# Four kinds of instruction get a larger margin in a list scheduler: squares of w2, splits of the signal, the gate's input, and the loads of the second feed-forward

## The chip, the cores and the metric

The kernel runs on one core of a Trainium2 chip. The metric is the device time of one launch in microseconds (us), the median of several runs. A core has five engines that each work through a queue of their own in the order in which the program was written: TensorE (PE, matrix products, with its weight loads shown apart as PEld), VectorE (DVE), ScalarE (ACT), GpSimd (POOL) and SyncE (SP). SP does no arithmetic here; it issues DMA transfers. POOL issues those transfers that add to what lies in DRAM. An instruction whose operand isn't there waits at the head of its queue, and everything behind it on that engine waits too.

## The reference

For x of shape 2048 x 1024 (sequence by features):

```
xn  = layernorm(x)
kv  = causal_conv4(k, shift_k) * v
y   = causal_conv2048(kv, ssm_k) + kv * ssm_D        # per feature, by FFT of length 4096
out = x + xn * y + silu(xn @ w1) @ w2                # w1: 1024 x 3584, w2: 3584 x 1024
```

All arrays are float32. The kernel computes its products with float16 pairs (a high and a low part), three matrix products for one.

## The kernel before, in words

**Two streams of work.** The feed-forward is nearly all of TensorE's work. Its first product (`steps`, lines 980 to 982) runs until 578 us, its second (`steps2`, lines 1123 to 1125) from 579.7 us to the end. For a large part of both a Strassen-Winograd scheme with seven products for eight is used (`units`, `units2`); between its products ScalarE and VectorE copy partial sums out of PSUM (`evacuate`, `evacuate2`), and TensorE can go on in a bank of PSUM only when the copy has been made. Beside it the long convolution runs in eight groups of 128 features: `gate` (short convolution and product with v), `signal_parts` (the signal is cut in four parts, each scaled and split into a float16 pair, and transposed by DMA), `stage1` (a first transform by matrix products, lines 1625 to 1627), `forward`, `product` and `inverse` (VectorE), `result_parts`, `stage1_inv` (lines 1813 to 1815) and `gated` (product with xn, then the output).

**The order is planned.** No engine's queue is written by hand. Some forty generators (`Stream`) offer operations (`Op`), each with an engine, an estimated duration and a margin. For the next operation of each stream the planner (`Order.prepare`, line 166) works out the time at which its operands are there by the plan's own estimates, and adds the margin:

```
s.at = max(t + op.margin, s.floor)      # line 176
t = max(self.free[s.head.eng], s.at)    # line 187
best = t - s.bias, t, s                 # line 189: the smallest t - bias is emitted next
```

So a margin removes and adds no instruction and no wait. It decides only how late in its engine's queue the operation is put: the planner takes it to be ready that much later, and other operations go in front. On the chip the operation starts when its engine comes to it and its semaphores allow it. The margins before the change are 0.15 us for an ACT instruction (`A`) and 0.3 us for a load (`L`).

**The four places that the change touches.**
- `square_w2` (line 1322): for each of 28 blocks of w2 (512 KB, loaded into one of two buffers, `wraw` and `w2n`) ScalarE squares the block and sums it up. A square frees its buffer for the next load. When all 28 are done, `norms_w2` (line 1327) derives the scale `tau`, and only then `load_w2` loads w2 again, to be split for the second product.
- `split` in `signal_parts` (line 1590): for seven of the eight groups, four parts each, ScalarE writes the high half into the tile `cm`, VectorE the low half, and SP issues two DMA transposes from `cm` into `sig`. There is one `cm`: a part's first instruction waits until the transposes of the part before have read it.
- `norm_rows` (line 1784): the gate's input, rows of x, is loaded into a tile of the ring `xg` (or into a free `ht`) by two transfers, and four ACT instructions of 128 x 128 subtract the mean. The next tile's loads are offered when these four have been emitted.
- `load_h` (line 1293): SP loads the activations of the first product, stored in DRAM, for the second: 160 tiles of `hs` and 56 of `hsf`, 256 KB each, into `wo`, twelve half tiles in turn. Each feeds twelve matmuls.

Of the kernel before, what the change touches and what calls it, by code (L numbers as in the profile page):

```python
# [15 lines left out]
AF = mybir.ActivationFunctionType  # L16
# [33 lines left out]
PRODUCTS = {"P1": ("A11", "B11"), "P7": ("S3", "T3"), "P6": ("S2", "T2"), "P2": ("A12", "B21"),  # L50
            "P5": ("S1", "T1"), "P3": ("S4", "B22"), "P4": ("A22", "T4")}
# [5 lines left out]
PLAIN = [j for j in range(NF) if j // 2 not in PAIRS]  # L57
# [62 lines left out]
class Order:  # L120
# [27 lines left out]
    def add(self, gen, bias, floor=0.0):  # L148
        s = Stream(gen, bias, floor)
        self.streams.append(s)  # L150
        self.advance(s)
# [151 lines left out]
def h3_ffn_kernel(ctx, tc, x, kp, vs, fs, shift, dskip, w1, w2, cfwd, cinv, out):  # L303
# [17 lines left out]
    def size(a):  # L321
        n = 1
        for s in a.shape[1:]:
            n *= s
        return n
# [4 lines left out]
    def A(f, o, ins, us=None, m=0.15):  # L330
        return Op("ACT", us or 1.02 * (0.16 + size(o) * 0.84e-3), 0.2, f, ins, [o], m)

    def T(f, o, ins, us, m=0.1):
        return Op("PE", us, 0.3, f, ins, [o], m)

    def L(o, i, m=0.3):
        n = size(o) * o.shape[0] * mybir.dt.size(o.dtype)
        return Op("SP", 0.4, 0.1, lambda: nc.sync.dma_start(o, i), [i], [o], m, n)

    def X(o, i, m=0.3, k=None):  # L340

        n = size(o) * o.shape[0] * mybir.dt.size(o.dtype)
        k = k or (1.2 if i.space == bass.MemoryType.DRAM else 3.0)
        return Op("SP", 0.65 + n / 240e3, 0.1, lambda: nc.sync.dma_start(o, i, transpose=True), [i], [o], m, k * n)
# [8 lines left out]
    def v_stt(o, a, s, b, op0, op1, **k):  # L353
        return V(lambda: nc.vector.scalar_tensor_tensor(o, a, s, b, op0=op0, op1=op1), o,  # L354
                 [a, b] + ([] if isinstance(s, float) else [s]), **k)

    def a_act(o, i, func, scale=1.0, bias=None, total=None):
        def f():
            kw = {} if bias is None else {"bias": bias}
            if total is not None:  # L360
                kw["accum_out"] = total
            nc.scalar.activation(o, i, func, scale=scale, **kw)  # L362
        ins = [i] + [s for s in (scale, bias) if s is not None and not isinstance(s, float)]
        p = A(f, o, ins)
        p.table = func if func in (AF.Silu, AF.Sqrt) else None
        p.busy += 0.07 * (len(ins) - 1) - 0.06 * (i.space == bass.MemoryType.PSUM)
        if total is not None:
            p.busy += 0.19
            p.writes.append(total)
        return p  # L370

    def split(hi, lo, src, scale, after=()):

        yield a_act(hi, src, AF.Copy, scale)
        yield v_stt(lo, src, scale, hi, MUL, SUB)
        for t in after:
            t.set()
# [3 lines left out]
    hsf = [{p[0]: dram.tile([4, P, NQ, 2, P], F16, name=f"hsf{p[0]}{b}") for p in PRODUCTS.values()} for b in range(2)]  # L381
    hs = [dram.tile([4, P, NF, 2, P], F16, name=f"hs{b}") for b in range(4)]
# [6 lines left out]
    mu = cst.tile([P, NT], F32, name="mu")  # L389
# [57 lines left out]
    def norm(ring, ss, ns, then, flags, margin=1.5):  # L447
# [27 lines left out]
        for t in flags[1]:  # L475
            t.set()


    def small(o, i, scale, ins=()):

        return Op("ACT", 0.2, 0.2, lambda: nc.scalar.activation(o, i, AF.Copy, scale=scale), [i, *ins], [o], 0.15)
# [110 lines left out]
    def turned(src, tok, name, i, bias):  # L592

        yield ft.ready
        pt, ptok = ft.tile([P, KH, P])

        def mm():
            for c in range(KH):
                nc.tensor.transpose(pt[:, c, :], src[:, c * P:(c + 1) * P], ident)
        yield T(mm, pt, [src], 0.44, m=0.3)  # L600
        flag["turned", name, i].set()
        if tok is not None:
            tok.set()
        o = factor(name)[:, i]
        after = (ptok, flag["x", 0, name]) + ((flag["rows", i],) if name in ("A11", "A12") else ())
        add(split(o[:, :, 0], o[:, :, 1], pt, XS, after), bias)
# [523 lines left out]
    def uses2():  # L1130

        yield 0, "P1"
        for u in range(len(tiles2)):
            for n in ("P7", "P6", "P2", "P5") if u + 1 < len(tiles2) else ("P6", "P7", "P5", "P2"):
                yield u, n
            if u + 1 < len(tiles2):
                yield u + 1, "P1"
            yield u, "P3"
            yield u, "P4"
# [153 lines left out]
    def load_h():  # L1293
        yield flag["factors"]
        for h in range(2):
            for c, t in [(c, t) for ts in TOGETHER[h] for c in range(NC) for t in ts]:
                yield wo.ready
                flag["h", h, t, c].what = o, _ = wo.tile([P, 4, 2, P], F16)
                yield L(o, hs[t // 4][t % 4][:, PLAIN[4 * c]:PLAIN[4 * c] + 4])
                flag["h", h, t, c].set()  # L1300
        for u, n in uses2():
            sp, q = tiles2[u]
            yield wo.ready
            flag["h2", u, n].what = o, _ = wo.tile([P, NQ, 2, P], F16)
            yield L(o, hsf[sp][PRODUCTS[n][0]][q])
            flag["h2", u, n].set()

    def squares_w2():
# [11 lines left out]
    flag["w2 squares"] = Token(2 * NP)  # L1320

    def square_w2(raw, tok, o):
        yield a_act(raw, raw, AF.Square, total=o)
        tok.set()
        flag["w2 squares"].set()

# [132 lines left out]
    def convolution(floor):  # L1459
# [3 lines left out]
        sp = ra.tile([P, 2, 8, 2, 2 * P], F32, name="spec")  # L1463
# [5 lines left out]
        acc = sig[:, 0]  # L1469
# [96 lines left out]
        def signal_parts():  # L1566

            for g in range(NG):
                yield flag["scales", g]
                kf, ktok = kfs[g]  # L1570
                sc, _ = scs[g]
                whole = [kparts[:, :, q].rearrange("p b t w -> p b (t w)") for q in range(2)]
                add(split(*whole, kf.rearrange("p b t w -> p b (t w)"), sc[:, 1:2], (ktok, flag["kparts", g])), CB)
                for t in TO:
                    there = acc16.rearrange("p b (i t) w -> p (b i) t w", i=2)[:, :, t]
                    two = [there[:, :, q * P:(q + 1) * P] for q in range(2)]
                    if g < BY_DMA:
                        yield py_r.ready
                        px, ptok = py_r.tile([P, 2, 2, P])

                        def mm():
                            for b in range(2):
                                for i in range(2):
                                    nc.tensor.transpose(px[:, b, i, :], acc[:, b, t + 4 * i, :], ident)
                        yield T(mm, px, [acc[:, :, t::4, :]], 0.44, m=2.0)
                        add(split(*two, px.rearrange("p b i w -> p (b i) w"), sc[:, 0:1], (ptok, flag["part", g, t])), CB)
                        continue
                    yield cm_r.ready
                    cm, ctok = cm_r.tile([P, 2, 2, 2, P], F16, 2)
                    yield from split(cm[:, 0], cm[:, 1], acc[:, :, t::4, :], sc[:, 0:1])  # L1590
                    flag["part", g, t].n = 2
                    for q, o in enumerate(two):
                        yield X(o, cm[:, q].rearrange("p b i w -> p (b i w)"))
                        ctok.set()
                        flag["part", g, t].set()
# [188 lines left out]
        def norm_rows():  # L1784

            for g in range(NG):
                for t in TO:
                    r = more["xg"]
                    yield lambda: r.ready() or flag["quads", 1]() and hts.ready()
                    xgs[g, t] = xg, _ = (r if r.ready() else hts).tile([P, 2, 2, P], uses=2)  # L1790
                    for b in range(2):
                        yield L(xg[:, b], x4[b][:, :, t, g * P:(g + 1) * P])
                    for b in range(2):
                        for i in range(2):
                            n = b * T2 + 4 * i + t
                            yield a_act(xg[:, b, i], xg[:, b, i], AF.Identity, -1.0, mu[:, n:n + 1])
                    flag["xg", g, t].set()

        def stage1_inv():
# [48 lines left out]
        for gen, bias in ((loads(), 0.05), (load_v(), 0.04), (gate(), 0.04), (signal_parts(), CB), (stage1(), 0.02),  # L1848
                          (transforms(), 0.02), (squares_w2(), 0.0), (rest(floor), 0.0)):
            add(gen, bias, floor)  # L1850
# [65 lines left out]
    add(feed_forward(), 0.0)  # L1916
    add(load_x(), 0.06)
    add(load_h(), 0.05)
    add(room(), 0.05)
    add(change(), 0.1)  # L1920
# [43 lines left out]
```

## Time and profile before

| | us |
|---|---|
| time, median of 3 runs (lowest, highest) | 1244.58 (1244.14, 1245.72) |
| the profiled execution's own time | 1244.12 |
| its span | 1242.0 |
| PE busy in the span | 1227.1 (99%) |
| DVE busy | 1107.2 (89%) |
| ACT busy | 775.7 (62%) |

The profile is that of one execution. The span goes from the first instruction to the last; 2.1 us of the execution's time lie around it. The granted clock of TensorE was full, 0.999 in the mean. A row of the timeline reads: start, duration, engine, line, operation, what it writes and reads, shapes; in brackets how long the engine had stood idle before it, and who ended that. A row of the waits reads: who waited for whom, then microseconds in total, how many times, and the longest. Most lines of ACT and DVE are those of a helper (362 for ACT, 354 and 351 for DVE, 338 for loads), so the names of the tiles tell the instructions apart.

### The profile page before, as it was taken

The page shows a single profiled execution, that of the slowest core. Times are in us where ns is not written, and L with a number is a line of the kernel's source. Part 1 is how long each engine was busy: PE and PEld are TensorE (multiplying, and loading weights), DVE is VectorE, ACT ScalarE, POOL GpSimd, SP SyncE. Part 2 cuts the span into 40 slices and gives each one's busy share as a digit, 9 for nine tenths or more (in the row PEclk, how much of TensorE's full clock was granted, in tenths as well). Part 3 has the DMA queues.
Part 4 walks back from the last instruction along what each step waited for, and adds up shares of the span by engine and source line. Part 5 has one row for each costly group of instructions (what it writes and reads, how often), then busy time and mean ns, then how long its engine had stood idle before and what let it go on. Part 6 is the DMA issues. An engine that isn't in the chain of part 4 may idle for free.

```text
span 1242.0 us, 16865 instructions
## 1 busy us (share of the span) xinstructions
PE 1227.1 (99%) x6044; PEld 596.2 (48%) x6044; DVE 1107.2 (89%) x1248; ACT 775.7 (62%) x1357; POOL 83.3 (7%) x93
## 2 busy tenths in 40 slices
PE   9999999999999999999999999999999999999998
PEld 8544444444444544445444544544444454444454
DVE  7999996996999779998899799899989979997981
ACT  7868997886688897559752732753363374554351
POOL 0000000000000000000000000001030130123123
PEclk9999999999999999999999999999999999999999
DMA  9598989899799899879986558489576784888776
GB/s 369 127 315 265 322 301 325 262 258 217 233 346 291 241 309 295 244 205 315 297 269 153 155 186 171 122 293 278 125 168 169 178 170 141 180 150 133 164 142 97
DMA packets 277700, 278.77 MB, mean 224 GB/s; under 512 B 85616, under 2 KB 204656, under 8 KB 276336
## 3 DMA queue, kind: packets, MB, share of 16 engines
q1 hardware_dynamic: 261888, 261.17, 70.2%
q0 software_dynamic: 15728, 16.52, 10.3%
q8 instruction: 47, 0.77, 0.3%
q14 instruction: 37, 0.30, 0.1%
HBM read 171.46 MB, written 88.34 MB: 209 GB/s over the span
## 4 chain that ended last, share of the span: by engine, by line
PE 70%; DVE 19%; DMA 4%; issue 3%; ACT 2%; SPq 0%; DVEq 0%; ACTq 0%
PE ff L980 10%; PE ff L981 10%; PE ff L982 10%; PE ff L1123 10%; PE ff L1124 10%; PE ff L1125 10%; DVE spec L351 7%; DVE tmp L351 2%; DVE wo L354 2%; DVE sig L354 1%; PE ps L1625 1%; PE ps L1627 1%; PE ps L1626 1%; DMA wraw<-in_w 1%; DVE x L354 1%
## 5 line engine op out<-in xcount | busy, mean ns | idle before, releaser
L1123 PE MATMUL ff<-x,wo 128*128 128x512 f16 x868 | 328.1, 378 | 2.0 <-ACT hf L362 0.9
L1125 PE MATMUL ff<-x,wo 128*128 128x512 f16 x868 | 328.1, 378 | 0.0
L1124 PE MATMUL ff<-x,wo 128*128 128x512 f16 x868 | 328.1, 378 | 0.0
L980 PE MATMUL ff<-x,wo 128*128 128x512 f16 (+1 forms) x808 | 302.8, 375 | 3.3 <-ACT hf L362 3.3
L982 PE MATMUL ff<-x,wo 128*128 128x512 f16 (+1 forms) x808 | 302.8, 375 | 0.0
L981 PE MATMUL ff<-x,wo 128*128 128x512 f16 (+1 forms) x808 | 302.8, 375 | 0.0
L351 DVE TENSOR_TENSOR spec<-spec 128x1024 f32<-128x1024 f32 (+2 forms) x232 | 259.3, 1146 | 2.0
L1125 PEld LDWEIGHTS <-wo 128*128 128x128 f16 x868 | 84.9, 98 | 101.6
L1124 PEld LDWEIGHTS <-wo 128*128 128x128 f16 x868 | 84.9, 98 | 101.3 <-issue 3.3
L1123 PEld LDWEIGHTS <-wo 128*128 128x128 f16 x868 | 85.8, 99 | 98.6
L982 PEld LDWEIGHTS <-wo 128*128 128x128 f16 x808 | 79.0, 98 | 92.4 <-DVE wo L354 0.5
L981 PEld LDWEIGHTS <-wo 128*128 128x128 f16 x808 | 79.0, 98 | 92.0 <-issue 3.9
L980 PEld LDWEIGHTS <-wo 128*128 128x128 f16 x808 | 80.5, 100 | 88.1
L351 DVE TENSOR_TENSOR tmp<-spec 128x2048 f32<-128x2048 f32 (+1 forms) x48 | 92.5, 1934 | 1.0
L354 DVE SCALAR_TENSOR_TENSOR ht<-hf,wsc,ht 128x1024 f16<-128x1024 f32 (+1 forms) x56 | 67.2, 1203 | 19.6 <-ACT ht L362 19.6
L362 ACT ACTIVATE spec<-spec 128x1024 bf16<-128x1024 f32 x32 | 33.7, 1053 | 59.6 <-DVE spec L351 59.5
L354 DVE SCALAR_TENSOR_TENSOR wo<-raw,wsc,wo 128x1024 f16<-128x1024 f32 (+1 forms) x56 | 63.9, 1147 | 4.4 <-ACT wo L362 4.0
L362 ACT ACTIVATE wo<-raw,wsc 128x1024 f16<-128x1024 f32 (+1 forms) x56 | 57.7, 1033 | 11.7 <-DVE raw L351 8.8
L354 DVE SCALAR_TENSOR_TENSOR sig<-kin,taps,sig 128x1024 f32<-128x1024 f32 x48 | 61.5, 1281 | 2.5 <-ACT sig L362 2.4
L348 POOL DMA_DIRECT2D out<-hf x44 | 39.3, 906 | 342.7 <-ACT hf L362 280.4
L351 DVE TENSOR_TENSOR spec<-tmp 128x512 f32<-128x512 f32 (+1 forms) x80 | 61.3, 794 | 1.1
L362 ACT ACTIVATE ht<-hf,wsc 128x1024 f16<-128x1024 f32 (+1 forms) x56 | 60.6, 1084 | 2.2 <-DVE hf L351 1.0
(191 smaller groups left out, 1695.3 us busy)
## 6 DMA issues: line engine op xcount, KB each, us to landing
wo<-hs SPq DMA_DIRECT2D x160, 256.0 KB, 3.6
hs<-ht SPq DMA_DIRECT2D x80, 256.0 KB, 4.7
raw<-in_w SPq DMA_DIRECT2D x28, 512.0 KB, 5.9
wraw<-in_w SPq DMA_DIRECT2D x24, 512.0 KB, 5.6
w2n<-in_w SPq DMA_DIRECT2D x24, 512.0 KB, 6.2
ws_T<-wo SPq DMA_DIRECT2D x22, 512.0 KB, 5.8
kin<-in_kp SPq DMA_DIRECT2D x16, 704.0 KB, 6.0
wo<-ws_T SPq DMA_DIRECT2D x22, 512.0 KB, 4.7
```

The source lines that it names most:

```text
L348: return Op("POOL", 1.1, 3.0, lambda: nc.gpsimd.dma_start(o, i, accum_op=ADD), [i], [o], m, 2.3 * n)
L351: return V(lambda: nc.vector.tensor_tensor(o, a, b, op=op), o, [a, b], **k)
L354: return V(lambda: nc.vector.scalar_tensor_tensor(o, a, s, b, op0=op0, op1=op1), o, [a, b] + ([] if isinstance(s, float) else [s]), **k)
L362: nc.scalar.activation(o, i, func, scale=scale, **kw)
L980: nc.tensor.matmul(o, w[:, 0, k], xf[:, :, k, 0], start=first and k == 0, stop=False, **kw)
L981: nc.tensor.matmul(o, w[:, 0, k], xf[:, :, k, 1], start=False, stop=False, **kw)
L982: nc.tensor.matmul(o, w[:, 1, k], xf[:, :, k, 0], start=False, stop=last and k == KH - 1, **kw)
L1123: nc.tensor.matmul(po, hx[:, n, 0, :], wc[:, n, 0, :], start=first and n == 0, stop=False, **kw)
L1124: nc.tensor.matmul(po, hx[:, n, 0, :], wc[:, n, 1, :], start=False, stop=False, **kw)
L1125: nc.tensor.matmul(po, hx[:, n, 1, :], wc[:, n, 0, :], start=False, stop=last and n == 3, **kw)
L1625: nc.tensor.matmul(o, cf[:, 0], h, start=i == 0, stop=False, **kw)
L1626: nc.tensor.matmul(o, cf[:, 0], l, start=False, stop=False, **kw)
```

## The change

Two things are added: a helper that raises an operation's margin, and an argument of `split` for it. Four kinds of operation get more margin: the squares of w2 4 us more, the high halves of `cm` 3 us more, the mean's subtraction in `norm_rows` 4 us more, and the loads of `load_h` 3.0 us in place of 0.3. The other uses of `split` keep their margin (`wait=0.0`).

```
-    def split(hi, lo, src, scale, after=()):
-        yield a_act(hi, src, AF.Copy, scale)
+    def split(hi, lo, src, scale, after=(), wait=0.0):
+        yield later(a_act(hi, src, AF.Copy, scale), wait)
...
+    def later(op, us):
+        op.margin += us
+        return op
...
     def load_h():
-                yield L(o, hs[t // 4][t % 4][:, PLAIN[4 * c]:PLAIN[4 * c] + 4])
+                yield L(o, hs[t // 4][t % 4][:, PLAIN[4 * c]:PLAIN[4 * c] + 4], 3.0)
...
-            yield L(o, hsf[sp][PRODUCTS[n][0]][q])
+            yield L(o, hsf[sp][PRODUCTS[n][0]][q], 3.0)
...
     def square_w2(raw, tok, o):
-        yield a_act(raw, raw, AF.Square, total=o)
+        yield later(a_act(raw, raw, AF.Square, total=o), 4)
...
     def signal_parts():
-                    yield from split(cm[:, 0], cm[:, 1], acc[:, :, t::4, :], sc[:, 0:1])
+                    yield from split(cm[:, 0], cm[:, 1], acc[:, :, t::4, :], sc[:, 0:1], wait=3)
...
         def norm_rows():
-                            yield a_act(xg[:, b, i], xg[:, b, i], AF.Identity, -1.0, mu[:, n:n + 1])
+                            yield later(a_act(xg[:, b, i], xg[:, b, i], AF.Identity, -1.0, mu[:, n:n + 1]), 4)
```

## The prediction

> **What bounds the kernel now.** I read the page's busy times first, then TensorE's waits.
>
> ```profile
> span 1242.0 us, 16865 instructions
> PE 1227.1 (99%) x6044; PEld 596.2 (48%) x6044; DVE 1107.2 (89%) x1248; ACT 775.7 (62%) x1357; POOL 83.3 (7%) x93
> ```
>
> ```profile
> PE ff L980 <- ACT hf L362: 3.3, 2, 2.3
> PE ft L599 <- DVE x L354: 1.9, 3, 1.2
> PE py L1814 <- DVE zl L354: 1.7, 3, 1.1
> PE ft L1891 <- DVE one L408: 1.2, 1, 1.2
> PE ff L1123 <- ACT hf L362: 0.9, 2, 0.5
> PE ft L599 <- DVE xt L580: 0.8, 1, 0.8
> PE ff L1123 <- DVE hf L354: 0.6, 1, 0.6
> PE ff L1123 <- ACT ff L362: 0.4, 1, 0.4
> PE py L1584 <- DVE sig L354: 0.4, 1, 0.4
> ```
>
> TensorE is busy for 1227.1 of 1242.0 us, and these nine rows are all its waits: 11.2 us. Nothing in the change shortens a matmul, so the time can fall only by what is in this list. The third thing to see is what the list lacks: TensorE never waits for a DMA. It waits for ACT and DVE, so a late transfer reaches it only through them. The rows of lines 599, 1891 and 1584 (4.3 us) belong to the start, ahead of any moved instruction. What the change can reach is 3.3 + 1.7 + 0.9 + 0.6 + 0.4 = 6.9 us.
>
> A wait counts for a little more than its row. Matmuls overlap, and the next rows, TensorE's timeline at its worst stop and at two others, show by how much.
>
> ```profile
> 337.86 0.38 PE L981 MATMUL ff<-x,wo 128*128 128x512 f16 x1
> 338.07 0.38 PE L982 MATMUL ff<-x,wo 128*128 128x512 f16 x1
> 340.74 0.38 PE L980 MATMUL ff<-x,wo 128*128 128x512 f16 x1 [2.28 <-ACT hf L362]
> ...
> 354.86 0.38 PE L980 MATMUL ff<-x,wo 128*128 128x512 f16 x1 [1.02 <-ACT hf L362]
> ...
> 1074.54 0.38 PE L1123 MATMUL ff<-x,wo 128*128 128x512 f16 x1 [0.41 <-ACT ff L362]
> ```
>
> Matmuls of 512 columns start 0.21 us apart (337.86, 338.07) though each is shown for 0.38. Without a stop the one at 340.74 would have come at 338.28; it lost 2.46, the idle 2.28 plus 0.17. I add 0.17 to every stop.
>
> **What ACT was doing then.** ACT's waits for transfers, and its timeline around the three stops:
>
> ```profile
> ACT cm L362 <- DMA sig<-cm: 24.7, 11, 5.9
> ACT ht L362 <- DMA ht<-in_x: 15.8, 6, 5.6
> ACT xg L362 <- DMA xg<-in_x: 12.6, 4, 6.2
> ACT wraw L362 <- DMA wraw<-in_w: 8.3, 5, 5.7
> ```
>
> ```profile
> 337.41 1.06 ACT L362 ACTIVATE wraw<-wraw 128x1024 f32<-128x1024 f32 x1 [5.74 <-DMA wraw<-in_w]
> 338.47 0.58 ACT L362 ACTIVATE ff<-ff 128x512 f32<-128x512 f32 x1
> ...
> 353.18 1.06 ACT L362 ACTIVATE wraw<-wraw 128x1024 f32<-128x1024 f32 x1 [0.61 <-DMA wraw<-in_w]
> ...
> 354.24 0.58 ACT L362 ACTIVATE hf<-ff 128x512 f32<-128x512 f32 x1
> ...
> 1067.60 0.72 ACT L362 ACTIVATE cm<-sig,csc 128x512 f16<-128x512 f32 x1 [1.96 <-DMA sig<-cm]
> ...
> 1073.92 0.57 ACT L362 ACTIVATE ff<-ff 128x512 f32<-128x512 f32 x1
> ```
>
> The first four rows are 61.4 us of ACT standing still for exactly the transfers that the change's ACT instructions read. Most of it costs nothing: ACT is 62% busy. Three of these waits had a copy out of PSUM behind them on which TensorE depended. At 331.7 ACT begins to wait 5.74 us for w2 to be squared, and behind that square (1.06 us, its sum besides) stands the copy of 338.47 (`ff<-ff`). At 353.18 the third square, after 0.61 of waiting, stands in front of the copy of 354.24. At 1067.60 ACT loses 1.96 us at `cm`, then works without a break to the copy of 1073.92; TensorE's stop there is shorter than that wait.
>
> **The change, part by part.** No instruction is added, removed or resized; busy times stay. What moves is 28 squares with their 28 sums, 128 subtractions on `xg` or `ht` (8 groups, 4 tiles, 4 each), 28 high halves of `cm`, and 216 loads on SP. With these go, later in the plan, what hangs on them: 28 low halves on DVE and 56 transposes on SP behind `cm`, the 28 loads of w2 (each needs the buffer that a square frees), and the 64 half loads of x. POOL's transfers are not moved by it; they are behind the convolution's last step, and I come to that under the rivals.
>
> *Squares and subtractions, at 331 to 355 us.* The squares go 4 us back; the copies of 338.47 and 354.24 pass them. Both stops fall away: (2.28 + 0.17) + (1.02 + 0.17) = 3.64 us.
>
> *`cm`, 3 us back.* The wait of 1.96 is passed by the copies behind it: 0.41 + 0.17 = 0.58 us. The other `cm`, `xg` and `ht` waits have no TensorE stop behind them: gain 0.
>
> *Loads of h, 2.7 us back.* No gain on TensorE, since it waits for no DMA. On SP they stop blocking others:
>
> ```profile
> SPq L338 <- PE ff L1125: 251.7, 140, 8.7
> ```
>
> ```profile
> wo<-hs SPq DMA_DIRECT2D x160, 256.0 KB, 3.6
> ```
>
> SP stands 140 times, 251.7 us in all, until a matmul frees a tile; transposes and other loads behind can now pass. That may shorten the waits above, which are already at zero in the sum: gain 0, and not a loss either. The cost side: twelve half tiles, each feeding twelve matmuls of 0.21 us, are a round of 31 us. Less 3.6 us to land, less the longest SP wait of 8.7, at least 18 us are left between landing and use. 2.7 us of them cost nothing.
>
> [...]
>
> *What covers the delays of the others.* These rows are the last square, tau, the first split of w2 that needs tau; the fourth `cm` of the tightest group, and the transform that reads it; the last subtraction of the first group and the product that uses it:
>
> ```profile
> 480.72 1.06 ACT L362 ACTIVATE w2n<-w2n 128x1024 f32<-128x1024 f32 x1 [0.29 <-DMA w2n<-in_w]
> ...
> 488.03 0.18 DVE L1343 TENSOR_SCALAR tau<-tau 128x14 f32<-128x14 f32 x1
> ...
> 553.94 1.15 ACT L362 ACTIVATE x<-wraw,tau 128x1024 f16<-128x1024 f32 x1 [0.84 <-PE ff L982]
> ...
> 979.02 0.71 ACT L362 ACTIVATE cm<-sig,csc 128x512 f16<-128x512 f32 x1
> ...
> 1005.19 0.38 PE L1625 MATMUL ff<-sig,cfw 128*128 128x512 f16 x1
> ...
> 384.18 0.97 ACT L362 ACTIVATE xg<-xg,mu 128x128 f32<-128x128 f32 x3
> ...
> 434.57 0.69 DVE L351 TENSOR_TENSOR xg<-py,xg 128x512 f32<-128x512 f32 x1
> ```
>
> ```profile
> DMA to landing us min/median/max: 2.4/3.6/8.9
> ```
>
> The squares run from 337 to 482 us through two buffers, 14 rounds. If each round grows by the whole 3.85 us, tau comes 54 us later, at 542. It is not used before 553.94, where ACT waited for TensorE and not for w2; with 6 us for loading, 60 of those 66 us are free. Cost 0, but not by much. `cm`: the four parts of a group are one chain, so the fourth comes up to 12 us later. In the tightest group 26.2 us lie between it and its matmul; less 2.7 for the two halves and the second transpose's issue, less 8.9 for the slowest landing (the row above is that of the transposes from `cm`), 14.6 are left. Cost 0. `xg`: four tiles in a chain, up to 16 us; 50 are there.
>
> **The sum.** 3.64 + 0.58 = 4.2 us less for the profiled execution: 1244.12 - 4.2 = 1239.9. The median of the runs lies 0.46 above that execution, so 1240.4. What is late next are stops that hang on VectorE's turn from one group to the next (the 1.7 us on `zl`) and the two of 0.9; I leave them as they are. Without any of the 6.9 us, with 0.17 for each of nine stops, 8.4 us would go; less the one of 0.6 + 0.17, which is the tail between the last two products and stays, 7.6: 1237.0, the low end. Upward, every queue after 331 us is dealt anew. A stop like the largest (2.45) that appears elsewhere costs its length; the sum's own range is one either way that stays faster, 1237.0 to 1242.0.
>
> **The rivals.**
>
> *Given back.* The new order puts other ACT or DVE work in front of PSUM copies; stops of the size of these return. For it: five of the nine stops have nothing to do with transfers and sit where the groups turn. Against: between 355 and 1060 us there are, with ACT waiting in nearly every window, only the `zl` stops. A move of 2 to 4 us given back is 1242.1 to 1247.0, no change that can be told: about 0.2%, 2.5 us, is what a measurement of this kernel can tell from none.
> [...]
>
> *The change doesn't do what it says.* If in the plan nothing else was ready, the moved instructions keep their places: 1244.6. Against it, at 338.47 a ready copy did stand behind.
>
> *Tau comes too late (slower).* If the rounds of squares grow not by 3.85 but by over 4.3 us (say because w2's loads fall behind loads of factors in SP's queue), tau passes 548 us, and the splits of w2, which feed the second product from 579.7 on, start late. TensorE takes the first block 25.7 us after that split (579.7 in the row below); loading and splitting a block fills some 12 of these (6 to land, four instructions of about 1.2), so 14 us more are hidden, and it decides from a round 5.3 us longer; at 5.8 it costs 14 x 0.5 = 7 us less the 4.2 gained: 1247.4.
>
> ```profile
> L1123 PE MATMUL ff<-x,wo x868: 269/379/380, 579.7 to 1237.9; 128*128 128x512 f16 x172, 128*128 128x256 f16 x2
> ```
>
> *The convolution ends late (slower).* The rows of its last output and of the last unit's copy:
>
> ```profile
> 1214.23 1.72 POOL L348 DMA_DIRECT2D out<-ht  x1
> ```
>
> ```profile
> 1224.72 0.69 ACT L362 ACTIVATE hf<-ff,invc 128x512 f32<-128x512 f32 x1 [4.49 <-PE ff L1125]
> ```
>
> The last unit loads back what the convolution added (flag `conv out`) right behind that copy. If the four `cm` of a group come over 14.6 us later, VectorE loses the rest in each group, and from 10.5 us in total TensorE's last products wait, us for us. Three us in six groups would be 18 - 10.5 - 4.2 = 3.3 us slower: 1247.9. Against: 12 is the plan's whole shift, and the waits of 24.7 us at `cm` are part of it already.
>
> *A load of h comes late.* It needs 16 us more than planned; a stop of that kind, once, is 1244 to 1256. Nothing in TensorE's list points to it.
>
> **How the numbers follow.** The sum 0.58; given back 0.17 and no effect 0.03; tau 0.09; convolution 0.08; new stops beyond what is gained, or a load of h, 0.05. So faster 0.58, same 0.20, slower 0.22. The range 1237.0 to 1248.0 takes in the sum, the middle and the nearer half of the slower cases.
>
> **What will show it.** Up to 331 us the two timelines should be the same. Right: no TensorE stop at 331 to 360, ACT waits for `wraw`, `xg`, `ht` and `cm` well under 61 us, ff L980 <- ACT near 0, tau between 490 and 545, the last output by POOL near 1214. Wrong: a DMA among TensorE's releasers, tau after 560, or new stops on `hf`, `ff` or `zl` that add up to over 4 us.

## The result, and the profile after

The changed kernel takes 1239.51 us (median of 6 runs, 1238.87 to 1242.08), the kernel before 1244.53 (6 runs): a ratio of 0.9959, with a 95% interval of 0.9943 to 0.9975. The forecast was 1240.4. The profiled execution of the changed kernel took 1241.13 us, 1.6 above the median, with a span of 1239.1; so the two profiles, 1242.0 and 1239.1, show only 2.9 of the 5 us.

The same views of the changed kernel. Its lines stand 3 to 5 lower in the file: 980 is 985, 1123 is 1128, 1814 is 1819. First the page, then TensorE's waits:

```profile
span 1239.1 us, 16865 instructions
PE 1226.6 (99%) x6044; PEld 595.9 (48%) x6044; DVE 1107.3 (89%) x1248; ACT 775.6 (63%) x1357; POOL 83.3 (7%) x93
```

```profile
PE py L1819 <- DVE zl L354: 1.8, 1, 1.8
PE ft L604 <- DVE x L354: 1.5, 2, 1.2
PE ft L604 <- DVE xt L585: 1.2, 1, 1.2
PE ft L1896 <- DVE one L408: 1.2, 1, 1.2
PE ff L985 <- ACT hf L362: 0.7, 1, 0.7
PE ff L1128 <- DVE hf L354: 0.6, 1, 0.6
PE py L1589 <- DVE sig L354: 0.4, 1, 0.4
PE ff L1128 <- ACT hf L362: 0.3, 1, 0.3
PE ff L985 <- DVE hf L351: 0.2, 1, 0.2
```

Every engine is busy for as long as before, to within 0.5 us. What shrank is the list: the rows of the start are still 4.3 us, the tail's is still 0.6, and of the 6.3 us between them 3.0 are left. The largest row of before, 3.3 on a copy by ACT at the first product, is 0.7.

Where that row came from, ACT's timeline again:

```profile
333.40 0.58 ACT L362 ACTIVATE ff<-ff 128x512 f32<-128x512 f32 x1 [0.71 <-PE ff L987]
335.93 0.69 ACT L362 ACTIVATE hf<-ff,wsc 128x512 f32<-128x512 f32 x1 [1.95 <-PE ff L987]
...
338.48 1.06 ACT L362 ACTIVATE wraw<-wraw 128x1024 f32<-128x1024 f32 x1 [0.68 <-DMA wraw<-in_w]
...
346.29 0.58 ACT L362 ACTIVATE hf<-ff 128x512 f32<-128x512 f32 x1
```

```profile
346.92 0.38 PE L985 MATMUL ff<-x,wo 128*128 128x512 f16 x1 [0.67 <-ACT hf L362]
```

The copy whose end ended the stop of before, from the timeline of that kernel:

```profile
340.02 0.67 ACT L362 ACTIVATE hf<-ff,wsc 128x512 f32<-128x512 f32 x1
```

The copy `ff<-ff`, which stood behind the first square at 338.47, now runs at 333.40, as soon as TensorE has made its input; the square comes after it and waits 0.68 us in place of 5.74. The next copy, `hf<-ff`, stood behind the first two squares at 340.02 and now runs at 335.93. The stop of 2.28 us is gone. A shorter one is new: a copy at 346.29 stands behind two instructions of the convolution.

Part of the gain is given back at one place. TensorE's and VectorE's timelines at the turn to the third group, first both of the changed kernel, then both of the kernel before:

```profile
684.25 0.27 PE L1818 MATMUL py<-zh,civ 128*128 128x256 f16 x1
686.33 0.27 PE L1819 MATMUL py<-zl,civ 128*128 128x256 f16 x1 [1.80 <-DVE zl L354]
```

```profile
684.99 2.48 DVE L354 SCALAR_TENSOR_TENSOR zl<-spec,csc,zh 128x1024 f16<-128x1024 f32 x2
```

```profile
687.10 0.27 PE L1813 MATMUL py<-zh,civ 128*128 128x256 f16 x1
687.67 0.27 PE L1814 MATMUL py<-zl,civ 128*128 128x256 f16 x1 [0.29 <-DVE zl L354]
```

```profile
686.33 2.48 DVE L354 SCALAR_TENSOR_TENSOR zl<-spec,csc,zh 128x1024 f16<-128x1024 f32 x2
```

TensorE comes to this place 2.85 us earlier than before (684.25 against 687.10), VectorE only 1.34 (684.99 against 686.33). So TensorE stands there for 1.80 us where it had stood for 0.29. VectorE is busy for 89% of the span, and at the groups' turns it is the engine that TensorE waits for (`zl`: 1.7 us in three stops before, 1.8 in one now).

### The profile page after: what moved, and what is told of

It is laid out like the page before. It is cut to its first block, busy times and chain, and to the rows that moved or that the text cites. A ratio compares the mean times of both kernels' runs of the same rounds, so it can differ in the third digit from the quotient of the medians.

```text
span 1239.1 us, 16865 instructions
## 1 busy us (share of the span) xinstructions
PE 1226.6 (99%) x6044; PEld 595.9 (48%) x6044; DVE 1107.3 (89%) x1248; ACT 775.6 (63%) x1357; POOL 83.3 (7%) x93
## 4 chain that ended last, share of the span: by engine, by line
PE 67%; DVE 21%; DMA 5%; issue 4%; ACT 2%; SPq 1%; DVEq 0%; ACTq 0%
PE ff L1128 11%; PE ff L1130 11%; PE ff L1129 11%; PE ff L985 8%; PE ff L986 8%; PE ff L987 8%; DVE spec L351 6%; DVE ht L354 2%; DVE tmp L351 2%; DVE x L354 2%; DVE sig L354 2%; DVE wo L354 2%; PE ps L1631 1%; PE ps L1630 1%; PE ps L1632 1%
```

## The experiments

Three theories. Theory 1 is the prediction's: what counts is a copy out of PSUM that stood behind an ACT instruction waiting for a transfer, so the squares carry the gain and the rest gives next to nothing. Theory 2: the loads of h, put later, unblock SP's queue and so bring all transfers earlier. Theory 3: any new order gains or loses a few us by chance.

The runs in one table. The third column is ACT's waits in the profile for the four kinds of transfer that the change concerns (`cm`, `xg`, `ht`, and the squares' `wraw` and `w2n`), the last what TensorE stood idle between 300 and 1226 us, summed over the rows of its waits. The first two rows are from the measurement above. The others were measured on three chips, each against the kernel before on the same chip, where that takes 1243.0 to 1243.1 us.

| what moves | ratio (interval) | ACT's waits, us | TensorE idle, us |
|---|---|---|---|
| nothing (before) | 1 | 61.7 | 6.3 |
| all four parts | 0.9959 (0.9943 to 0.9975) | 16.9 | 3.0 |
| all four parts, again | 0.9963 (0.995 to 0.9977) | 20.6 | 1.8 |
| squares by 4 | 0.9966 (0.9954 to 0.9978) | 53.7 | 2.2 |
| first four squares by 4 | 0.9981 (0.9969 to 0.9993) | 56.1 | 3.0 |
| squares by 2 | 1.0004 (0.9991 to 1.0016) | 52.8 | 5.9 |
| squares and subtractions by 4 | 0.9956 (0.9942 to 0.997) | 24.6 | 0.4 |
| subtractions by 4 | 0.9998 (0.9988 to 1.0009) | 35.7 | 5.6 |
| `cm` by 3 | 1.0004 (0.9995 to 1.0014) | 43.8 | 5.3 |
| loads of h by 2.7 | 1.0018 (1.001 to 1.0027) | 64.6 | 7.5 |
| loads of h by 5.7 | 0.9997 (0.9988 to 1.0007) | 66.3 | 4.8 |
| all but the squares | 1.0018 (1.0008 to 1.0028) | 18.7 | 6.0 |
| squares by 10 | 1.0299 (1.0284 to 1.0315) | 67.0 | 38.6 |
| squares by 4, `cm` by 9 | 1.0072 (1.0058 to 1.0085) | 41.7 | 2.2 (a stop of 10.1 comes after 1226) |

**Each part alone.** Four kernels, in each of which one of the four margins is that of the changed kernel and the others are those of before:

```
 sq_only:  later(a_act(raw, raw, AF.Square, total=o), 4)                           # the rest 0, 0, 0.3
 xg_only:  later(a_act(xg[:, b, i], ..., AF.Identity, -1.0, mu[:, n:n + 1]), 4)
 cm_only:  split(cm[:, 0], cm[:, 1], ..., sc[:, 0:1], wait=3)
 h_only:   L(o, hs[...], 3.0) and L(o, hsf[...], 3.0)
```

> Only the squares of w2 keep their 4 us; the other three have the margins of before. Theory 1 (the gain is the copies out of PSUM that stood behind a square): both stops of 331 to 355 us go, 3.6 us less than before, about 1240.9; ACT's wait for wraw falls from 8.3 to under 2 us. Theory 2 (the gain is SP's queue, unblocked by the later loads of h): about 1244.5. Theory 3 (any new order gains or loses a few us by chance): anything within 4 us of before, and the four single parts don't add up to the 5.0 us of all.

> Only the subtractions on xg and ht keep their 4 us. Theory 1: no TensorE stop stood behind one of them, so within 1 us of before, 1243.5 to 1245.5, though ACT's waits for xg and ht fall from 28.4 us to a few. Theory 2: no change. Theory 3: up to 4 us either way.

> Only the high halves of cm keep their 3 us. Theory 1: one stop of 0.58 us goes, about 1244.0. Theory 2: no change, 1244.5. Theory 3: up to 4 us either way.

> Only the loads of h keep their margin of 3.0 us. Theory 1: 0, about 1244.5; SP's wait for PE at line 338 falls well under 251.7 us. Theory 2: most of the 5.0 us gained, about 1240, by shorter ACT waits for transfers. Theory 3: up to 4 us either way.

The squares alone give 0.34%, 4.2 us, all of the change's gain within the intervals. TensorE's waits after 300 us in that kernel, the tail left out, have no row at the first product:

```profile
PE py L1819 <- DVE zl L354: 0.7, 1, 0.7
PE ps L1630 <- ACT tmp L362: 0.6, 1, 0.6
PE ff L1128 <- ACT hf L362: 0.4, 1, 0.4
PE ps L1630 <- DVE tmp L351: 0.3, 1, 0.3
PE ff L1128 <- DVE hf L354: 0.2, 1, 0.2
```

Subtractions and `cm` alone make no difference, though ACT's waits fall from 61.7 to 35.7 and 43.8 us. The loads of h alone cost 0.18%, 2.2 us. TensorE's three largest waits in that kernel:

```profile
PE ff L985 <- ACT hf L362: 3.1, 2, 2.6
PE py L1819 <- DVE zl L354: 1.9, 1, 1.9
PE py L497 <- ACT spec L362: 1.6, 1, 1.6
```

The first row is the old stops, the other two are new or larger. The timelines of ACT, VectorE and TensorE at the third, all of the kernel with the loads of h alone:

```profile
882.14 0.72 ACT L362 ACTIVATE cm<-sig,csc 128x512 f16<-128x512 f32 x1 [3.90 <-DMA sig<-cm]
883.33 1.06 ACT L362 ACTIVATE spec<-spec 128x1024 bf16<-128x1024 f32 x1 [0.47 <-DVE spec L351]
```

```profile
882.00 1.29 DVE L351 TENSOR_TENSOR spec<-tmp 128x512 f32<-128x512 f32 x2
```

```profile
884.53 0.39 PE L497 MATMUL py<-css,one 128*128 128x4 f32 x2 [1.56 <-ACT spec L362]
```

A small matmul of the convolution needs ACT's sum of squares of the product (`spec`), and the whole of the second product stood behind this matmul in TensorE's queue. In ACT's queue the sum stands behind a `cm` that waited 3.90 us, but that isn't what held it: after the `cm` ACT stood idle for 0.47 us more, until VectorE had made `spec` at 883.29. VectorE has no row in this kernel's list of waits between 870 and 900 us. So this stop is not of the kind that the change takes away; TensorE came ahead of VectorE, as at `zl`.

Theory 2 falls: SP's wait at line 338 for a matmul of the second product fell from 251.7 to 191.1 us, and nothing was gained. Theory 3 is not out: the single ratios add up to -0.14%, the four together give -0.41 and -0.37. With the intervals of the four parts that sum is uncertain by some 0.2% either way, so the difference lies at the edge of the noise.

**All but the squares, and the loads of h by more.**

```
 no_sq:  cm 3, subtractions 4, loads of h 3.0, squares 0
 h_6:    only the loads of h, 6.0 in place of 3.0
```

> The changed kernel with the squares back at their old margin; cm, xg and h keep theirs. If the squares carry the gain (they gave 3.7 us alone): both or most of the 3.6 us of stops at 331 to 355 us return and the time is that of before within 1.5 us. If the other three carry something together that none shows alone (the four single ratios add up to -0.14%, all four together to -0.41%): 2 to 4 us faster than before. By the h part's own theory (loads of h later make ACT wait longer for the transposes from cm, 37.5 us against 24.7, unless cm moves too) the ACT wait for cm is under 20 us here.

> Only the loads of h move, by 5.7 us in place of 2.7 (2.7 alone: 2.3 us slower than before). If the loss comes with the delay (ACT's wait for cm, or a late load): larger, 3 to 6 us slower. If it was the chance of one order: anything between 2 us faster and 3 slower, and not larger with the margin. SP's wait for PE at line 338 falls below 191 us.

Without the squares nothing is gained; 0.18%, 2.2 us, is lost, somewhat more than the 1.5 us that I had allowed, though ACT's waits are at 18.7 us, among the lowest of all. TensorE's list doesn't show where (6.0 us against 6.3); the profiled execution, 1243.53 us, was one of the shortest of this kernel, 1.7 below its median. So the three parts don't carry the gain in company either, and the sum of ACT's waits says nothing about the time: 53.7 us of them are left in the kernel with the squares alone, which is as fast as the whole change. With the loads of h moved by twice as much the loss of 0.18% isn't there. So it doesn't come with the delay, nor with ACT's wait for `cm`, which is 37.8 us here and was 37.5 in the kernel that lost. That it was the chance of one order is what is left, and isn't shown. SP's wait fell further, to 149.1 us, and again nothing was gained.

**Two smaller doses of the squares.**

```
 sq_first:  later(..., 4) for the first four squares, 0 for the other 24
 sq_2:      later(..., 2) for all 28
```

> Only the first four of the 28 squares move, by 4 us; all else has the margins of before. Theory 1 (the gain is the two stops at 338 and 353 us, behind the first and third square): the whole gain of the squares, 3.6 us, and tau within 10 us of 488, not 527. If the gain is spread over the squares, or comes from the later loads of w2 that a later square brings: under half of it, 1.8 us.

> All 28 squares move by 2 us in place of 4. The first copy stood behind a wait of 5.74 us and the third square's behind 0.61: by theory 1 both copies pass if the plan has them ready within 2 us of the square, 3.6 us faster; if only the second passes, 1.2 us faster.

Four squares of 28 are enough to take both stops of 331 to 355 us away; the kernel's waits after 300 us have no row of the first product left, and tau comes only 5.4 us later than before:

```profile
PE py L1819 <- DVE zl L354: 1.9, 3, 1.0
PE ff L1128 <- ACT hf L362: 0.8, 2, 0.5
PE ps L1630 <- DVE spec L351: 0.3, 1, 0.3
```

```profile
493.39 0.17 DVE L1348 TENSOR_SCALAR tau<-tau 128x14 f32<-128x14 f32 x1
```

The time falls by 0.19%, 2.4 us, with an interval of 0.9 to 3.9. That is less than the 3.6 that I expected, more than the half that would have spoken for the other 24 squares, and settles it only as far as the profile does: the two stops go, and of the 3.0 us that are left 1.9 are at `zl`, at the groups' turns. Why the order with all 28 moved has less left (2.2) is not explained; I take it for theory 3.

The prediction and the expectation call the square at 353.18 the third. It is the third in `wraw`, but the fifth in all: before, ACT squares at 337.41, 338.98, 342.94, 349.99 and 353.18. So it has no margin in this kernel. It comes later all the same, at 358.87, behind the four that were moved, and the copy `hf<-ff` runs ahead of it at 349.46.

The two stops are also not equally firm. The kernels with `cm` alone and with the loads of h alone, by 2.7 and by 5.7, have ACT's instructions up to 355 us in the same order as before. The first stop is 2.28 us before and 2.10, 2.62 and 1.73 in these three. The second is 1.02 before and 0, 0.47 and 0.41 in these (with `cm` alone TensorE had run at a granted clock of 0.50 between 343 and 346 us, see the last section). In the two other kernels that leave the squares (subtractions alone, all but the squares) the first is 2.58 and 1.75 and the second is gone. In none of the eight kernels that move squares is more than 0.2 us of the first left. So the first stop is shown to hang on the squares; the second comes and goes without them.

Two us for all 28 is an example of how a new order deals other stops. The stops of 331 to 355 us shrink to one of 0.2 us, as expected, but the expected 3.6 us don't come. What was gained is lost again at the turns (2.8 us at `zl`) and at the end of the first product (1.4 us at 577):

```profile
PE py L1819 <- DVE zl L354: 2.8, 2, 2.0
PE ff L985 <- DVE hf L351: 1.4, 1, 1.4
PE ff L1128 <- ACT hf L362: 1.1, 2, 0.8
PE ff L1128 <- ACT ff L362: 0.4, 1, 0.4
PE ff L985 <- ACT hf L362: 0.2, 1, 0.2
```

**The two slower rivals, forced.**

```
 sq_10:    only the squares, 10 in place of 4
 sq4_cm9:  squares 4, cm 9 in place of 3
```

> Only the squares move, by 10 us in place of 4. The prediction's tau rival: each of 14 rounds may grow by 9.85 us, tau comes up to 138 us later (488 to 626) and from 5.3 us a round on it costs: up to 64 us slower, and TensorE stands in front of line 1128 for splits of w2. In the changed kernel 4 us made the squares 39 us longer (184 against 145), 2.8 a round; in that proportion 10 us give 7 a round, tau near 586 and 24 us slower. If the cover is larger than I worked out: as fast as squares alone by 4, 1239 to 1241.

> Squares by 4 us and the high halves of cm by 9 in place of 3; xg and h as before. The prediction's convolution rival: the fourth part of a group comes up to 36 us later against a cover of 14.6 in the tightest group, VectorE loses up to 21 us there and 10.5 us more are hidden at the end; with one or two such groups 5 to 30 us slower than squares alone (1239.3). If the plan fills the shift with the room of other groups: within 3 us of squares alone.

Squares by 10 us cost 3.0%, 37 us. Tau and TensorE's waits:

```profile
615.62 0.17 DVE L1348 TENSOR_SCALAR tau<-tau 128x14 f32<-128x14 f32 x1
```

```profile
PE py L457 <- DVE q L1340: 26.6, 1, 26.6
PE ff L1128 <- ACT x L362: 6.5, 2, 4.5
PE ff L1129 <- DVE x L354: 3.4, 2, 1.9
```

Tau comes 127.6 us after that of before, so a round grew by 9.1 us: of a margin of 10 us nearly all goes into the round, of 4 us (all four parts) only 2.8. The first row is a wait that I had not seen: TensorE itself makes a small matmul for the norm (line 457), it stands in TensorE's queue at its planned place ahead of the second product, and TensorE stood 26.6 us in front of it. The splits that come late, the prediction's form of this rival, cost the other two rows.

`cm` by 9 us costs 13.7 us over the squares alone (1253.0 against 1239.32, on another chip). POOL's last outputs of the convolution, the one large row of TensorE's waits, and the copy by ACT that it waited for:

```profile
1233.48 2.32 POOL L348 DMA_DIRECT2D out<-ht  x2 [0.23 <-issue]
```

```profile
PE ff L1128 <- ACT ht L362: 10.1, 1, 10.1
```

```profile
1238.40 1.26 ACT L362 ACTIVATE ht<-ff,invc 128x512 f32<-128x512 f32 x2 [7.05 <-DMA out<-ht]
```

The last such issue was at 1214.23 before; it is about 20 us later here, some 10 were hidden at the end and 10.1 are a stop of TensorE in its last products. That agrees with the prediction's cover of 10.5 us. The delay is the convolution's: the last group's first `zl` comes at 1218.44, with the squares alone at 1201.21. But it reaches TensorE by another way than the prediction said. By the profile it wasn't the loading back that the last unit waited for; its copy goes into a tile `ht` that the convolution's output transfer was still reading. The rest of the 13.7 us is in part a lower clock behind this stop (0.50 between 1239 and 1242 us, last section).

**All four again, and squares with subtractions.**

```
 all_four:  the changed kernel
 sq_xg:     squares 4, subtractions 4, cm 0, loads of h 0.3
```

> The changed kernel once more, on one chip with the next three. If the three other parts add nothing to the squares: a ratio near 0.9966, that of the squares alone; if they add something in company: 0.995 or below.

> Squares and subtractions move by 4 us, cm and h as before. By theory 1 as squares alone, 3.7 us faster than before, within 1.5 us; ACT's waits for xg and ht fall from 31.9 us (squares alone) to under 8.

The whole change gives 0.9963, and the squares alone gave 0.9966, on another chip, each against the kernel before on its own chip: the other three parts add nothing that can be told. Squares with subtractions had the lowest median, 1238.27 us, and a TensorE that stands idle for 0.4 us between 300 and 1226; the intervals of the three overlap, so it isn't shown to be better. With 0.4 us left in that list, hardly more is to be had by taking away stops of TensorE in this part of the kernel.

## Why the prediction was right, point by point

- *The bound.* TensorE's list of waits was the right thing to read. Before and after it has the same 6044 matmuls, the other kernels differ from these in margins alone, and the spans follow the stops: the span less all rows of TensorE's waits is 1230.5 to 1232.4 us in eleven kernels. In the other three, where the mean granted clock was 0.998, 0.995 and 0.983, it is 1233.2, 1233.9 and 1237.0.
- *Squares, 3.64 us.* Right in kind: 0.34% alone, 4.2 us with an interval of 2.7 to 5.7; both stops go, and moving the first four squares suffices for that. But 1.19 of the 3.64 is the second stop, which other executions have smaller or not at all with the squares unmoved. One sign was not met in full: there is still a stop of 0.67 us at 346.92. The subtractions, put into the same term, have no share in it (0.9998 alone).
- *`cm`, 0.58 us.* Not found: 1.0004 alone. It is too small for its interval (0.9995 to 1.0014) to decide. The stop itself, 0.41 us at 1074.54, is gone in every other kernel but the one with the squares by 2, also in those that leave `cm` at its old margin; so that term of the sum has no support from a run.
- *Loads of h, 0.* SP's wait fell as said, and brought nothing. Alone they cost 2.2 us, a loss that the step had excluded. The lateness of a load explains little of it: the profile has one TensorE wait of 0.3 us for `wo`, and at 5.7 us the loss is gone. Its cause stays open.
- *Given back.* The largest stop after the change is this rival's: 1.8 us at `zl`, where TensorE arrives ahead of VectorE. The prediction had named the `zl` stops as late next and left their size as it was (1.7 in three stops); it came out at 1.8 in one. Between orders the stops after 360 us vary by more than I allowed, from 0.4 us (squares and subtractions) to 5.7 (squares by 2).
- *Tau.* Said: between 490 and 545 us, cost nothing. Measured: 526.93, no stop. (`later` adds its 4 us to the old margin, so a round could have grown by 4, not 3.85, and tau have come at 544; nothing else changes by this.) The price of the rival was oversized: by my 60 + 14 = 74 us of cover, the 127.6 us of delay would have cost 54. It cost 42 over the squares by 4, 37 over the kernel before, and the largest part of it by another wait than the one I had in mind.
- *Convolution.* Said: last output near 1214. Its last output but one was issued at 1215.17, the last only at 1220.88, and cost no stop. The forced kernel shows the rival's cover and price about as worked out, by another way to TensorE.
- *ACT's waits well under 61 us.* They are 16.9, and that was no test of anything: with the squares alone they are 53.7 at the same time.
- *The number.* 1240.4 was forecast and 1239.5 measured; that they lie so close is in part luck. Of the 4.2 us in the sum, the 2.45 of the first stop are shown to hang on the squares. The 0.58 has no support, the 1.19 comes and goes, and what the new order adds and takes away at other places is as large as these terms.

## What to carry to other kernels

On an engine that is far from full (ACT, 62% busy here), the sum of its waits is worth nothing (16.9 and 53.7 us of them went with the same time); what counts is which waits have, behind them in the same queue, an instruction that the full engine needs. Here one of 27 did for certain, a second in some executions, and moving four instructions by 4 us took both away. Before a wait is moved or a margin raised, follow the order of the full engine's releasers; and expect that any new order of a planned kernel deals its small stops anew (between 300 and 1226 us they add up to 4.8 to 7.5 us in the five kernels that keep the squares' old margin, against 6.3 before), so that a part's worth has to be measured alone and in company.

## What the runs showed of the hardware

**After a short stop TensorE ran at half its clock for a while in one kernel, and not in three others that had one.** In the kernel with `cm` alone, the old stop of 338 us (2.10 us idle by the profile) was followed by matmuls at half pace. Its timeline, and the granted clock in windows (the third-last number of a row):

```profile
342.34 0.38 PE L985 MATMUL ff<-x,wo 128*128 128x512 f16 x1 [2.10 <-ACT hf L362]
...
342.77 0.52 PE L987 MATMUL ff<-x,wo 128*128 128x512 f16 x1
343.09 0.63 PE L985 MATMUL ff<-x,wo 128*128 128x512 f16 x1
343.52 0.63 PE L986 MATMUL ff<-x,wo 128*128 128x512 f16 x1
```

```profile
336.00:340.00 4.00, 4.00 (x20) 1.82 (x19) 4.00 (x4) 0.98 (x2) 0.00 (x0) 1.00 0.80 280
343.00:346.00 3.00, 3.00 (x8) 1.06 (x7) 2.49 (x2) 3.00 (x8) 0.00 (x0) 0.50 1.01 326
```

The granted clock was 0.50 between 343 and 346 us, and matmuls started 0.43 us apart, against 0.22 ahead of the stop (339.21, 339.43). Stops of 2.3 to 2.6 us at the same place in three other kernels (before, loads of h alone, subtractions alone) had no such sequel: the granted clock was 1.00 in the windows around them. Behind the longest stops of the forced kernels, 10.1 and 26.6 us, it was 0.50 too (between 1239 and 1242 us, and between 618 and 623). What decides isn't shown: of these four stops the one with the sequel was the shortest, 2.10 us against 2.28, 2.58 and 2.62.

**A stop that comes and goes.** Ahead of anything that the change moves, all these kernels have the same order, yet one stop near 198 us came out between nothing and 1.38 us. With `cm` alone:

```profile
197.92 1.06 ACT L362 ACTIVATE junk<-raw 128x1024 bf16<-128x1024 f32 x1 [4.11 <-DMA raw<-in_w]
```

```profile
199.69 0.38 PE L985 MATMUL ff<-x,wo 128*128 128x512 f16 x1 [1.38 <-ACT x L362]
```

In the profile of before, the same instruction waited 2.54 us and TensorE not at all. It is one more square in front of a copy that TensorE needs, in the first product. It may account for a part of the spread between runs of one kernel; that wasn't measured.
